# Windowed attention before a softmax-gated layer: four groups of partitions hold half a sequence of one head instead of a quarter of two

## The chip, the cores and the metric

The kernel runs on one core of one Trainium2 chip. The metric is the device time of one execution in microseconds (us); the kernel before takes 502.13 us, the median of three runs (501.51 to 502.85).

## The reference, cut to what matters

There are 8 batches of 8 heads, 576 positions and 64 numbers per head. Each query sees 32 keys behind it: the nearest 32 in heads 0 to 3, every fourth of the last 128 in heads 4 to 7. The attention output, 4608 rows of 512, then goes through a dense layer to 1024, a softmax-weighted gate, a normalisation and a dense layer back to 512.

```python
mask_plain = (rel >= 0) & (rel < window)                                   # window = 32
mask_dil = (rel >= 0) & (rel < window * dilation) & (rel % dilation == 0)  # dilation = 4
attn = softmax(where(mask, q @ k.T / 8, -1e9)); x = attn @ v               # per batch and head
h = x @ w_in;  e = exp(h - max(h));  solu = h * e / sum(e)
out = ((solu - mean) / sqrt(var + 1e-6) * g_ln) @ w_out
```

The host reorders the positions of the dilated heads by their remainder by four, so both kinds of head become a window of 32 neighbours, in the dilated case with three class borders at which the window is cut.

## The kernel before, in words

The attention is done in 32 units, one for each batch and pair of heads (`NUNIT`). Units with n % 4 below 2 are plain, the others dilated. The dense layers are done in 36 tiles of 128 tokens. The order of the work on each engine is written out by hand: the string `OPENING` gives it for the first part, `STEP` and `AMID` for tiles 6 to 15, `PAIR` and its variants for the pairs of tiles after that. A word such as `S5` is "the scores of unit 5"; each word issues its instructions on its engine at that place. All loads go through SP's queue in the order of the words.

A unit's words are these. `q` and `v` load its operands. `S` (`scores`, L235 to L259) multiplies queries and keys on TensorE. The 576 queries of a head are cut into four groups of 144, each group into five blocks of 32 (the last block of a group is half used), and a block is multiplied with 64 keys. Head h lies in partitions 64h to 64h+63 of both operands, group c is written to partitions 32c to 32c+31, head h to its own PSUM bank: 5 x 2 x 4 = 40 matmuls, each 64 rows by 32 columns of the array, with 64 columns streamed. For units 0 to 9 (`PE_MASK`) two matmuls with an identity first write the mask into the banks; for the others `mask` adds it on VectorE (L266). Then come `max`, `sub`, `exp`, `sum`, `inv`, `norm` and `turn` (a 32x32 transpose), all on tiles of 128 x 640. `sub` is on GpSimd except in the early units, `exp` on ScalarE, `norm` on GpSimd for units 0 to 9, the rest on VectorE. `V` (`attend`, L318 to L337) multiplies the turned probabilities with the values: one matmul for each 32-key block (six in a group, five where the first is left out), each group and each head, 32 rows by 64 columns of the array, with 16 to 64 columns streamed; group c writes bank 4 + c. A plain unit has 48 of them, a dilated one 40. `xh` and `xl` copy the result out of PSUM (L366, L368, L385).

The scores of units 0 to 4 use banks 2 and 3, which the dense layer's odd tiles use too; those of later units use columns 144 to 463 of banks 6 and 7, whose first 144 columns belong to `V`.

The profile shows two records for each fp32 matmul of `S` and `V`, and two weight loads: an fp32 matmul is done in two passes with the same operands.

The lines of `S` and `V` that set which part of the array works:

```python
for i in range(NS):                      # S
    for h in range(2):
        for c in range(NG):
            out=ps[WIN * c : WIN * c + WIN, h, WQ * i : WQ * i + WQ]
            lhsT=qt[D * h : D * h + D, q0 : q0 + WIN]
for i in range(first, NV):               # V
    for c in range(NG):
        for h in range(2):
            out=ps_x[D * h : D * h + D, c, c0 : c0 + k1 - k0]
            lhsT=vt[WIN * c : WIN * c + WIN, i, D * h : D * h + D]
```

Of the kernel before, what the change touches and what calls it, by code (L numbers as in the profile page):

```python
# [9 lines left out]
F32 = mybir.dt.float32  # L10
# [19 lines left out]
NG = P // WIN  # L30
GQ = S // NG
NS = -(-GQ // WIN)
NV = NS + 1
SPAN = GQ * (NG - 1) + WIN * NS
RING = 2 * S
# [14 lines left out]
OPENING = (  # L50
# [72 lines left out]
LAST_BANKS = {NTILE - 3: 0, NTILE - 1: 1}  # L123
OFFSET = {'qt2': 48, 'kt2': 32, 'vt2': 48, 'qt3': 48, 'kt3': 48, 'vt3': 48}
SLOTS = "t0 t1 t2 t3 raw4 raw5 tp t0 t1 t2 t3 raw4 raw5 tp t3 tp".split()
MERGED = 5
SHIFT = {}
# [3 lines left out]
def windowed_attention_then_solu_kernel(  # L131
# [38 lines left out]
    banks = psum.tile([P, 8, 512], F32, name="banks")  # L170
    ps_x = banks[:, 4:8, 0:GQ]

# [9 lines left out]
    def ps_s(n):
        if n < MERGED:
            return banks[:, 2:4, 0 : NS * WQ]
        return banks[:, 6:8, GQ : GQ + NS * WQ]

# [9 lines left out]

    setup.tile([P, 48], F32, name="before_mag")
    loaded = {}

    def load_qk(n):  # L200

        if n >= NUNIT:
            return
        qt = units.tile([P, SPAN], F32, name=f"qt{buf(n)}", bufs=1)
        kt = units.tile([P, WIN + SPAN], F32, name=f"kt{buf(n)}", bufs=1)
# [29 lines left out]
    def scores(n):  # L235

        qt, kt = loaded[n]["q"], loaded[n]["k"]
        dil = int(n % NPAIR >= NPAIR // 2)
        ps = ps_s(n)
        st[n] = {"ps": ps.rearrange("p h (s w) -> p h s w", w=WQ)}  # L240
        on_pe = n in PE_MASK
        if on_pe:
            for h in range(2):
                nc.tensor.matmul(  # L244
                    out=ps[:, h, :], lhsT=id_bf, rhs=mask_sb[:, dil, :],
                    start=True, stop=False, skip_group_check=True,
                )
        for i in range(NS):
            for h in range(2):
                for c in range(NG):  # L250
                    q0 = GQ * c + WIN * i
                    nc.tensor.matmul(  # L252
                        out=ps[WIN * c : WIN * c + WIN, h, WQ * i : WQ * i + WQ],
                        lhsT=qt[D * h : D * h + D, q0 : q0 + WIN],
                        rhs=kt[D * h : D * h + D, q0 : q0 + WQ],
                        start=not on_pe,
                        stop=True,
                        skip_group_check=True,
                    )  # L259

    def soft_mask(n):
        if n in PE_MASK:
            return
        dil = int(n % NPAIR >= NPAIR // 2)
        sm = st[n]["sm"] = att.tile([P, 2, NS, WQ], F32, name=f"sm{n % 2}")
        nc.vector.tensor_tensor(  # L266
            out=sm.rearrange("p h s w -> p h (s w)"), in0=ps_s(n),
            in1=mask_sb[:, dil, :].unsqueeze(1).broadcast_to([P, 2, NS * WQ]),
            op=ALU.add,
        )  # L270

    def wide(x):
        return x.unsqueeze(3).broadcast_to([P, 2, NS, WQ])

    def soft_max(n):
        mx = st[n]["mx"] = small.tile([P, 2, NS], F32, name="mx")
        src = st[n]["ps"] if n in PE_MASK else st[n]["sm"]
        nc.vector.tensor_reduce(out=mx, in_=src, axis=AX.X, op=ALU.max)  # L278

    def soft_copy(n):  # L280
        sm = st[n]["sm"] = att.tile([P, 2, NS, WQ], F32, name=f"sm{n % 2}")
        nc.scalar.copy(out=sm, in_=st[n]["ps"])

# [27 lines left out]
    def turn(n):  # L311

        pt = st[n]["pt"] = att.tile([P, 2, NS * WQ], F32, name=f"pt{n % 2}")
        nc.vector.transpose(
            out=pt.rearrange("p h w -> p (h w)"), in_=st[n]["sm"].rearrange("p h s w -> p (h s w)")
        )
# [531 lines left out]
    def conv_lo(b):  # L848
# [149 lines left out]
```

## Time and profile before

| | |
|---|---|
| time, median of three runs | 502.13 us |
| span of the profiled execution | 501.3 us |
| busy: TensorE matmuls / weight loads | 471.7 / 379.3 us |
| busy: VectorE, ScalarE, GpSimd | 351.9, 289.1, 295.7 us |
| moved by DMA | 94.07 MB, 188 GB/s on average |

The span goes from the first to the last instruction of the profiled execution; the page gives no other time of that execution, and its span lies 0.8 us below the median of the runs. In the views, PE is TensorE's matmuls, PEld its weight loads, DVE is VectorE, ACT ScalarE, POOL GpSimd, SP the engine that issues the loads. PEclk is the share of TensorE's full clock that was granted (1.00 is 2.4 GHz, 0.50 is 1.2 GHz).

### The profile page before, as it was taken

The page shows a single profiled execution, that of the slowest core. Times are in us where ns is not written, and L with a number is a line of the kernel's source. Part 1 is how long each engine was busy: PE and PEld are TensorE (multiplying, and loading weights), DVE is VectorE, ACT ScalarE, POOL GpSimd, SP SyncE. Part 2 cuts the span into 40 slices and gives each one's busy share as a digit, 9 for nine tenths or more (in the row PEclk, how much of TensorE's full clock was granted, in tenths as well). Part 3 has the DMA queues.
Part 4 walks back from the last instruction along what each step waited for, and adds up shares of the span by engine and source line. Part 5 has one row for each costly group of instructions (what it writes and reads, how often), then busy time and mean ns, then how long its engine had stood idle before and what let it go on. Part 6 is the DMA issues. An engine that isn't in the chain of part 4 may idle for free.

```text
span 501.3 us, 16598 instructions
## 1 busy us (share of the span) xinstructions
PE 471.7 (94%) x7088; PEld 379.3 (76%) x7088; DVE 351.9 (70%) x619; ACT 289.1 (58%) x481; POOL 295.7 (59%) x367
## 2 busy tenths in 40 slices
PE   3449988999999999999999999999999999999997
PEld 2337766888887888878778787878787888888876
DVE  3998897768446788787868686868676864445562
ACT  3756986645233445444457575757575767666552
POOL 0463774575344665778976666665757555766440
PEclk9999997999999999999999999999999999999999
DMA  8999637554347555565667677776765545454461
GB/s 283 349 377 346 190 78 252 150 177 154 112 130 226 179 174 162 171 194 169 200 170 221 199 218 205 214 209 211 212 211 164 161 129 147 104 157 141 109 181 70
DMA packets 50905, 94.07 MB, mean 188 GB/s; under 512 B 5648, under 2 KB 25616, under 8 KB 50832
## 3 DMA queue, kind: packets, MB, share of 16 engines
q1 hardware_dynamic: 49968, 92.30, 59.8%
q8 instruction: 55, 0.90, 0.7%
q10 hardware_dynamic: 864, 0.72, 0.4%
q14 instruction: 18, 0.15, 0.1%
HBM read 59.97 MB, written 28.31 MB: 176 GB/s over the span
## 4 chain that ended last, share of the span: by engine, by line
PE 87%; DVE 8%; DMA 2%; issue 2%; ACT 1%; SPq 0%; DVEq 0%; ACTq 0%
PE banks L528 37%; PE banks L758 20%; PE banks L398 17%; PE banks L330 6%; PE banks L252 6%; DMA t<-w_in 1%; PE banks L549 1%; DVE mag L821 1%; DVE mag L836 1%; DVE t L433 1%; DVE mx L278 1%; DVE rs L299 1%; DVE low L828 1%; DMA mid<-t 1%; PE banks L244 0%
## 5 line engine op out<-in xcount | busy, mean ns | idle before, releaser
L528 PE MATMUL banks<-w_o,th 128*128 128x512 f32 x560 | 174.9, 393 | 0.0
L528 PEld LDWEIGHTS banks<-w_o,th 128*128 128x128 f32 x560 | 103.6, 188 | 21.8 <-ACT th L513 0.4
L519 POOL TENSOR_TENSOR tl<-t,th 128x512 fp32r<-128x512 f32 x68 | 88.1, 1310 | 48.4 <-ACT th L513 48.1
L528 PE MATMUL banks<-w_o,tl 128*128 128x512 f32 x280 | 109.3, 390 | 0.0
L398 PE MATMUL banks<-w_i,x_hi 128*128 128x512 f32 x256 | 84.0, 410 | 0.1
L528 PEld LDWEIGHTS banks<-w_o,tl 128*128 128x128 f32 x280 | 52.5, 188 | 11.6 <-DVE tl L519 0.4
L513 ACT CAST th<-t 128x512 fp32r<-128x512 f32 x72 | 43.5, 620 | 28.3 <-DVE t L505 14.6
L398 PEld LDWEIGHTS banks<-w_i,x_hi 128*128 128x128 f32 x256 | 48.3, 195 | 11.1 <-DVE mu L433 0.2
L505 DVE STREAM_TRANSPOSE t<-raw 128x512 f32<-128x512 f32 x72 | 47.4, 687 | 10.4 <-DMA raw<-mid 10.3
L398 PE MATMUL banks<-w_i,x_lo 128*128 128x512 f32 x128 | 51.3, 401 | 0.0
L330 PEld LDWEIGHTS banks<-pt,vt 32*64 32x64 f32 x2816 | 35.2, 137 | 20.9 <-issue 10.5
L449 ACT ACTIVATE e<-t 128x1024 f32<-128x1024 f32 x35 | 37.0, 1057 | 21.4 <-DVE t L445 21.0
L330 PE MATMUL banks<-pt,vt 32*64 32x64 f32 (+3 forms) x2816 | 38.7, 234 | 9.9 <-DMA vt<-vw 4.0
L291 POOL TENSOR_TENSOR sm<-sm,mx 128x640 f32<-128x640 f32 x25 | 31.6, 1263 | 24.2 <-DVE mx L278 17.0
L266 DVE TENSOR_TENSOR sm<-banks,packed 128x640 f32<-128x640 f32 x22 | 18.1, 823 | 38.8 <-PE banks L252 38.8
L295 ACT ACTIVATE sm<-sm 128x640 f32<-128x640 f32 x32 | 23.6, 738 | 35.0 <-POOL sm L291 32.4
L252 PEld LDWEIGHTS banks<-kt,qt 64*32 64x32 f32 x2560 | 29.9, 113 | 16.1 <-issue 9.8
L540 ACT ACTIVATE ob<-banks,rstd 128x512 f32<-128x512 f32 x35 | 24.0, 686 | 27.9 <-issue 16.7
L252 PE MATMUL banks<-kt,qt 64*32 64x64 f32 x2560 | 35.7, 241 | 4.0 <-DMA qt<-qT 3.2
L782 DVE CUSTOM_DVE_ANT_0 t<-banks,t 128x512 f32<-128x512 f32 x30 | 20.7, 690 | 22.4 <-PE banks L758 17.0
L776 ACT COPY t<-banks 128x512 f32<-128x512 f32 x30 | 17.6, 588 | 30.3 <-PE banks L758 30.3
L442 ACT ACTIVATE t<-t,mu 128x1024 f32<-128x1024 f32 x23 | 26.4, 1149 | 11.0 <-DVE mu L441 11.0
(156 smaller groups left out, 880.0 us busy)
## 6 DMA issues: line engine op xcount, KB each, us to landing
mid<-t SPq DMA_DIRECT2D x140, 128.0 KB, 2.4
raw<-mid SPq DMA_DIRECT2D x34, 512.0 KB, 3.8
vt<-vw SPq DMA_DIRECT2D x32, 384.0 KB, 3.9
kt<-kT SPq DMA_DIRECT2D x32, 312.0 KB, 4.0
qt<-qT SPq DMA_DIRECT2D x32, 296.0 KB, 4.3
out<-ob SPq DMA_DIRECT2D x35, 256.0 KB, 2.6
x_hi<-x SPq DMA_DIRECT2D x12, 288.0 KB, 3.6
t<-w_in SPq DMA_DIRECT2D x5, 512.0 KB, 8.4
```

The source lines that it names most:

```text
L252: nc.tensor.matmul(out=ps[WIN * c : WIN * c + WIN, h, WQ * i : WQ * i + WQ], lhsT=qt[D * h : D * h + D, q0 : q0 + WIN], rhs=kt[D * h : D * ...
L291: eng.tensor_tensor(out=st[n]["sm"], in0=st[n]["sm"], in1=wide(mx), op=ALU.subtract)
L330: nc.tensor.matmul(out=ps_x[D * h : D * h + D, c, c0 : c0 + k1 - k0], lhsT=vt[WIN * c : WIN * c + WIN, i, D * h : D * h + D], rhs=pt[WIN * ...
L398: nc.tensor.matmul(out=ps_h(i)[:, half], lhsT=a[:, kt, xs], rhs=w_i[:, kt, half, part, :], start=(kt == 0 and k == 0), stop=(kt == KT - 1 ...
L442: nc.scalar.activation(out=dst, in_=src, func=AF.Identity, bias=mu, scale=1.0)
L449: nc.scalar.activation(out=e, in_=t, func=AF.Square, accum_out=per_tile(i, "sq"))
L505: nc.vector.transpose(out=turned(i)[:, cut(c)].rearrange("p k (a r) -> p k a r", r=WIN), in_=ms[i]["mv"].rearrange("p (a k s) -> p k a s", ...
L513: nc.scalar.copy(out=ms[i]["th"][:, cut(c)], in_=turned(i)[:, cut(c)])
L519: eng.tensor_tensor(out=ms[i]["tl"][:, cut(c)], in0=turned(i)[:, cut(c)], in1=ms[i]["th"][:, cut(c)].bitcast(F32), op=ALU.subtract,)
L528: nc.tensor.matmul(out=ps_o(i), lhsT=a[:, f, :], rhs=w_o[:, f, part, :], start=(f == 0 and k == 0), stop=(f == FT - 1 and k == 2), skip_gr ...
L540: nc.scalar.activation(out=ob, in_=ps_o(i), func=AF.Copy, scale=rstd)
L758: nc.tensor.matmul(out=banks[:, bank], lhsT=left(pa, kt), rhs=right(pb, kt), start=j in (1, 2, 5) and kt == 0 and k == 0, stop=kt == 1 and ...
```

## The change: nine whole blocks of one head in each group

The 576 queries of a head are now cut into two halves of 288, which are nine whole blocks of 32. Group c of 32 partitions holds half c % 2 of head c // 2. So a unit's score tile is 128 x 576 instead of 128 x 640. `S` has 9 x 2 x 2 = 36 matmuls instead of 40. `V` has 38 in a plain unit instead of 48 (ten key blocks in the second half, nine in the first, whose first block lies before the sequence), and 36 in a dilated unit instead of 40. Head h in partitions 64h to 64h+63 now meets only groups 2h and 2h+1.

The scores of all units use columns 192 to 511 of bank 6 (five blocks) and 0 to 255 of bank 7 (four). The value products use columns 0 to 287 of banks 4 and 5, one bank for each half. The mask is no longer shared by the two heads, so the packed constants grow from 392 to 648 columns; they are loaded in two pieces, the identity and the plain mask first (352 columns), the dilated mask and the gains (296 columns) by a new word `rest` between `S1` and `q2`. The padding of queries, keys and values goes: q has 576 columns instead of 592, k 608 instead of 624, v 640 instead of 768.

```diff
-GQ = S // NG
-NS = -(-GQ // WIN)
+GQ = S // 2
+NS = GQ // WIN
+FIRST_BANK = 5
-    "pack q0 S0 w0 q1 max0 sub0 low0 abs0 w3 exp0 abs3 S1 q2 clamp0 low3 sign0 sum0 w2 inv0 "
+    "pack q0 S0 w0 q1 max0 sub0 low0 abs0 w3 exp0 abs3 S1 rest q2 clamp0 low3 sign0 sum0 w2 inv0 "
-    ps_x = banks[:, 4:8, 0:GQ]
+    ps_x = banks[:, 4:6, 0:GQ]
+    s0 = 7 * 512 - FIRST_BANK * WQ
+    ps_s = banks.rearrange("p a b -> p (a b)")[:, s0 : s0 + NS * WQ]
-        vt = units.tile([P, NV, 2 * D], F32, name=f"vt{buf(n)}", bufs=1)
+        vt = units.tile([P, NV, D], F32, name=f"vt{buf(n)}", bufs=1)
...
         for i in range(NS):
-            for h in range(2):
-                for c in range(NG):
-                    q0 = GQ * c + WIN * i
+            for half in range(2):
+                for h in range(2):
+                    c = 2 * h + half
+                    q0 = GQ * half + WIN * i
                     nc.tensor.matmul(
-                        out=ps[WIN * c : WIN * c + WIN, h, WQ * i : WQ * i + WQ],
+                        out=ps_s[WIN * c : WIN * c + WIN, WQ * i : WQ * i + WQ],
...
-        for i in range(first, NV):
-            k0, k1 = max(WQ * i - WIN, 0), min(WQ * i + WIN, WQ * NS - WQ + WIN + GQ % WIN)
+        for i in range(NV):
+            k0, k1 = max(WQ * i - WIN, 0), min(WQ * i + WIN, NS * WQ)
             c0 = WIN * max(i - 1, 0)
-            for c in range(NG):
+            for half in range(2):
+                first = int(dil or half == 0)
+                if i < first:
+                    continue
                 for h in range(2):
+                    c = 2 * h + half
                     nc.tensor.matmul(
-                        out=ps_x[D * h : D * h + D, c, c0 : c0 + k1 - k0],
-                        lhsT=vt[WIN * c : WIN * c + WIN, i, D * h : D * h + D],
-                        rhs=pt[WIN * c : WIN * c + WIN, h, k0:k1],
+                        out=ps_x[D * h : D * h + D, half, c0 : c0 + k1 - k0],
+                        lhsT=vt[WIN * c : WIN * c + WIN, i, :],
+                        rhs=pt[WIN * c : WIN * c + WIN, k0:k1],
...
-        "pack": lambda _: nc.sync.dma_start(out=packed, in_=pack),
+        "pack": lambda _: nc.sync.dma_start(out=packed[:, 0:early], in_=pack[:, 0:early]),
+        "rest": lambda _: nc.sync.dma_start(out=packed[:, early:], in_=pack[:, early:]),
```

## Rows read from the trace of the kernel before

**Rows 1.** The page, part 4: the chain that ended last, by engine.

```profile
PE 87%; DVE 8%; DMA 2%; issue 2%; ACT 1%; SPq 0%; DVEq 0%; ACTq 0%
```

**Rows 2.** Windows: stretch, its length, busy us (instructions) of PE, PEld, DVE, ACT, POOL; PEclk, DMA, GB/s.

```profile
25.00:50.00 25.00, 17.62 (x455) 14.11 (x456) 22.84 (x36) 15.57 (x26) 12.12 (x10) 1.00 0.97 362
50.00:75.00 25.00, 22.86 (x581) 17.91 (x580) 23.05 (x40) 23.02 (x37) 18.39 (x28) 0.99 0.47 134
75.00:100.00 25.00, 23.23 (x244) 18.50 (x243) 18.77 (x32) 16.72 (x28) 13.59 (x16) 0.87 0.64 199
300.00:325.00 25.00, 25.00 (x410) 20.15 (x408) 18.48 (x38) 16.06 (x29) 16.50 (x22) 1.00 0.73 211
```

**Rows 3.** Chain in order of time, 300 to 345 us: start, length, what.

```profile
299.93 1.01 PE banks L330 x70
...
303.89 0.97 PE banks L252 x64
...
325.24 1.13 PE banks L330 x75
```

**Rows 4.** Waits of PE after 90 us, all of them: total us, times, longest.

```profile
PE banks L549 <- DVE tl L519: 0.2, 1, 0.2
PE banks L330 <- issue: 0.2, 1, 0.2
```

**Rows 5.** Timeline of PE around one `S`: start, first start to last end, records.

```profile
380.14 1.04 PE L252 MATMUL banks<-kt,qt 64*32 64x64 f32 x80
381.11 0.50 PE L758 MATMUL banks<-tp,w_i 128*128 128x512 f32 x1
```

**Rows 6.** Windows on L252, same `S`: PE and PEld records begun by each end; PEclk.

```profile
380.13:380.19 0.06, 0.05 (x8) 0.05 (x12) 1.00 0.76 307
380.13:380.22 0.09, 0.08 (x8) 0.08 (x16) 1.00 0.76 307
380.13:380.27 0.14, 0.13 (x16) 0.13 (x23) 1.00 0.76 307
380.13:380.33 0.20, 0.19 (x24) 0.19 (x32) 1.00 0.87 353
```

**Rows 7.** Windows on L252, an `S` at half clock.

```profile
84.89:84.95 0.06, 0.05 (x8) 0.05 (x12) 0.50 0.01 0
84.89:85.10 0.21, 0.20 (x16) 0.20 (x24) 0.50 0.00 0
84.89:85.20 0.31, 0.30 (x24) 0.30 (x32) 0.50 0.00 0
```

**Rows 8.** Windows on L330, a plain `V`.

```profile
388.00:388.08 0.08, 0.07 (x8) 0.07 (x11) 1.00 0.00 0
388.00:388.14 0.14, 0.13 (x16) 0.13 (x20) 1.00 0.00 0
388.00:388.22 0.22, 0.21 (x24) 0.21 (x31) 1.00 0.00 0
```

**Rows 9.** Groups of instructions by line: busy us, mean ns, idle before and releaser.

```profile
L266 DVE TENSOR_TENSOR sm<-banks,packed 128x640 f32<-128x640 f32 x22 | 18.1, 823 | 38.8 <-PE banks L252 38.8
L278 DVE TENSOR_REDUCE mx<-sm 128x10 f32<-128x640 f32 x22 | 18.0, 820 | 0.8
L314 DVE STREAM_TRANSPOSE pt<-sm 128x640 f32<-128x640 f32 x32 | 26.8, 837 | 0.9 <-POOL sm L309 0.6
L505 DVE STREAM_TRANSPOSE t<-raw 128x512 f32<-128x512 f32 x72 | 47.4, 687 | 10.4 <-DMA raw<-mid 10.3
```

**Rows 10.** Chain in order of time, 0 to 112 us, four of 129 pieces.

```profile
33.11 1.41 PE banks L252 x80
...
36.87 1.46 PE banks L330 x62
...
63.01 0.84 DVE mx L278
...
84.97 1.33 PE banks L252 x78
```

**Rows 11.** DMA issues: times, KB each, median us to landing.

```profile
vt<-vw SPq DMA_DIRECT2D x32, 384.0 KB, 3.9
...
packed<-pack SPq DMA_DIRECT2D x1, 196.0 KB, 2.4
```

More of the change, by code (lines that the diff above doesn't have):

```diff
@@ L123 @@
 LAST_BANKS = {NTILE - 3: 0, NTILE - 1: 1}
[L124 removed]
+OFFSET = {'qt2': 48, 'kt2': 48, 'vt2': 112, 'qt3': 48, 'kt3': 48, 'vt3': 112}
 SLOTS = "t0 t1 t2 t3 raw4 raw5 tp t0 t1 t2 t3 raw4 raw5 tp t3 tp".split()
[L126 removed]
 SHIFT = {}
@@ L161, in windowed_attention_then_solu_kernel @@
     id_bf = packed[:, 0 : P // 2].bitcast(BF16)
+    early = P // 2 + NS * WQ // 2
     mask_sb = packed[:, P // 2 : P // 2 + NS * WQ].bitcast(BF16).rearrange("p (d c) -> p d c", d=2)
@@ L180, in ps_o @@
         return banks[:, LAST_BANKS.get(i, i % 2 if i < PAIRED - 2 else 3)]
[L182 to L185, printed above, removed]
     nc.vector.memset(mhalf, -0.5)
@@ L195, in buf @@
         return n % 4 if n < 12 else n % 2
-    setup.tile([P, 48], F32, name="before_mag")
+    setup.tile([P, 112], F32, name="before_mag")
+    units.tile([P, 64], F32, name="before_units", bufs=1)
     loaded = {}
@@ L203, in load_qk @@
             return
-        qt = units.tile([P, SPAN], F32, name=f"qt{buf(n)}", bufs=1)
-        kt = units.tile([P, WIN + SPAN], F32, name=f"kt{buf(n)}", bufs=1)
+        qt = units.tile([P, S], F32, name=f"qt{buf(n)}", bufs=1)
+        kt = units.tile([P, WIN + S], F32, name=f"kt{buf(n)}", bufs=1)
         nc.sync.dma_start(out=kt, in_=kT[n])
@@ L238, in scores @@
         dil = int(n % NPAIR >= NPAIR // 2)
-        ps = ps_s(n)
-        st[n] = {"ps": ps.rearrange("p h (s w) -> p h s w", w=WQ)}
+        st[n] = {"ps": ps_s.rearrange("p (s w) -> p s w", w=WQ)}
         on_pe = n in PE_MASK
         if on_pe:
-            for h in range(2):
+            for cols in (slice(0, FIRST_BANK * WQ), slice(FIRST_BANK * WQ, NS * WQ)):
                 nc.tensor.matmul(
-                    out=ps[:, h, :], lhsT=id_bf, rhs=mask_sb[:, dil, :],
+                    out=ps_s[:, cols], lhsT=id_bf, rhs=mask_sb[:, dil, cols],
                     start=True, stop=False, skip_group_check=True,
@@ L264, in soft_mask @@
         dil = int(n % NPAIR >= NPAIR // 2)
-        sm = st[n]["sm"] = att.tile([P, 2, NS, WQ], F32, name=f"sm{n % 2}")
+        sm = st[n]["sm"] = att.tile([P, NS, WQ], F32, name=f"sm{n % 2}")
         nc.vector.tensor_tensor(
-            out=sm.rearrange("p h s w -> p h (s w)"), in0=ps_s(n),
-            in1=mask_sb[:, dil, :].unsqueeze(1).broadcast_to([P, 2, NS * WQ]),
-            op=ALU.add,
+            out=sm.rearrange("p s w -> p (s w)"), in0=ps_s, in1=mask_sb[:, dil, :], op=ALU.add
         )
     def wide(x):
-        return x.unsqueeze(3).broadcast_to([P, 2, NS, WQ])
+        return x.unsqueeze(2).broadcast_to([P, NS, WQ])
     def soft_max(n):
-        mx = st[n]["mx"] = small.tile([P, 2, NS], F32, name="mx")
+        mx = st[n]["mx"] = small.tile([P, NS], F32, name="mx")
         src = st[n]["ps"] if n in PE_MASK else st[n]["sm"]
@@ L280, in soft_copy @@
     def soft_copy(n):
-        sm = st[n]["sm"] = att.tile([P, 2, NS, WQ], F32, name=f"sm{n % 2}")
+        sm = st[n]["sm"] = att.tile([P, NS, WQ], F32, name=f"sm{n % 2}")
         nc.scalar.copy(out=sm, in_=st[n]["ps"])
@@ L286, in soft_sub @@
         if n in PE_MASK and n not in ACT_SCORES:
-            sm = st[n]["sm"] = att.tile([P, 2, NS, WQ], F32, name=f"sm{n % 2}")
+            sm = st[n]["sm"] = att.tile([P, NS, WQ], F32, name=f"sm{n % 2}")
             nc.vector.tensor_tensor(out=sm, in0=st[n]["ps"], in1=wide(mx), op=ALU.subtract)
@@ L297, in soft_sum @@
     def soft_sum(n):
-        rs = st[n]["rs"] = small.tile([P, 2, NS], F32, name="rs")
+        rs = st[n]["rs"] = small.tile([P, NS], F32, name="rs")
         nc.vector.tensor_reduce(out=rs, in_=st[n]["sm"], axis=AX.X, op=ALU.add)
@@ L311, in turn @@
     def turn(n):
[L313 to L316, printed above, removed]
+        pt = st[n]["pt"] = att.tile([P, NS * WQ], F32, name=f"pt{n % 2}")
+        nc.vector.transpose(out=pt, in_=st[n]["sm"].rearrange("p s w -> p (s w)"))
     def attend(n):
@@ L344, in x_order @@
         if n % NPAIR < NPAIR // 2:
-            return x.rearrange("p (c i) -> p c i", c=NG)
-        return x.rearrange("p (i c) -> p i c", c=NG)
+            return x.rearrange("p (b i) -> p b i", b=2)
+        return x.rearrange("p (i b c) -> p i b c", b=2, c=2)
     def x_view(n, x):
@@ L351, in from_v @@
     def from_v(n):
-        return ps_x if n % NPAIR < NPAIR // 2 else ps_x.rearrange("p c i -> p i c")
+        if n % NPAIR < NPAIR // 2:
+            return ps_x
+        return ps_x.rearrange("p b (c i) -> p i b c", c=2)
     def whole(n):
@@ L561, in moe_out_part @@
         else:
-            ob = att.tile([P, 2, NS, WQ], F32, name=f"sm{int(on_act)}")
-            ob = ob.rearrange("p h s w -> p (h s w)")
+            ob = att.tile([P, NS, WQ], F32, name=f"sm{int(on_act)}")
+            ob = ob.rearrange("p s w -> p (s w)")
         rows, rstd = out[i * P : i * P + P, :], ms[i]["rstd"]
@@ L613, in in_unit @@
     def in_unit(name):
-        shape = {"q": [P, SPAN], "k": [P, WIN + SPAN], "v": [P, NV, 2 * D], "x": [P, S]}[name[0]]
+        shape = {"q": [P, S], "k": [P, WIN + S], "v": [P, NV, D], "x": [P, S]}[name[0]]
         pool = att if name == "x" else units
@@ L936, in _mask @@
         for p in range(P):
-            q0 = GQ * (p // WIN) + WIN * s
+            q0 = GQ * (p // WIN % 2) + WIN * s
             q = q0 + p % WIN
             k = q0 - WIN + c
-            ok = (q >= S) | ((k >= 0) & (q - k >= 0) & (q - k < WIN))
+            ok = (k >= 0) & (q - k >= 0) & (q - k < WIN)
             m[p, 0, s, ok] = 0.0
-            m[p, 1, s, ok & ((q >= S) | (k // CLS == q // CLS))] = 0.0
+            m[p, 1, s, ok & (k // CLS == q // CLS)] = 0.0
     return m.reshape(P, 2, NS * WQ)
@@ L961 @@
     q, k, v = (np.concatenate([a[:, :hh], _class_major(a[:, hh:])], axis=1) for a in (q, k, v))
-    qT = np.zeros((NUNIT, P, SPAN), q.dtype)
-    qT[:, :, :S] = q.reshape(NUNIT, 2, S, D).transpose(0, 1, 3, 2).reshape(NUNIT, P, S)
-    kT = np.zeros((NUNIT, P, WIN + SPAN), k.dtype)
-    kT[:, :, WIN : WIN + S] = k.reshape(NUNIT, 2, S, D).transpose(0, 1, 3, 2).reshape(NUNIT, P, S)
-    vp = np.zeros((NUNIT, WIN + SPAN, 2, D), v.dtype)
-    vp[:, WIN : WIN + S] = v.reshape(NUNIT, 2, S, D).transpose(0, 2, 1, 3)
-    vw = np.stack([vp[:, GQ * c : GQ * c + WIN * NV] for c in range(NG)], axis=1)
-    vw = vw.reshape(NUNIT, NG, NV, WIN, 2 * D).transpose(0, 1, 3, 2, 4)
-    vw = np.ascontiguousarray(vw).reshape(NUNIT, P, NV, 2 * D)
+    qT = q.reshape(NUNIT, 2, S, D).transpose(0, 1, 3, 2).reshape(NUNIT, P, S)
+    qT = np.ascontiguousarray(qT)
+    kT = np.zeros((NUNIT, P, WIN + S), k.dtype)
+    kT[:, :, WIN:] = k.reshape(NUNIT, 2, S, D).transpose(0, 1, 3, 2).reshape(NUNIT, P, S)
+    vp = np.zeros((NUNIT, 2, WIN + S, D), v.dtype)
+    vp[:, :, WIN:] = v.reshape(NUNIT, 2, S, D)
+    vw = np.stack([vp[:, :, GQ * c : GQ * c + WIN * NV] for c in range(2)], axis=2)
+    vw = vw.reshape(NUNIT, NG, NV, WIN, D).transpose(0, 1, 3, 2, 4)
+    vw = np.ascontiguousarray(vw).reshape(NUNIT, P, NV, D)
     arrays = {
```

6 lines of the change are left out of this document (1 added, 5 removed).

## The prediction

> **What bounds the kernel now.** Read the chain of waits first: TensorE holds 87% of it [rows 1]. Then the windows, since the share is an average: between 25 and 75 us VectorE is busy 22.8 to 23.1 of 25 us while TensorE has idle time, and up to 50 us the DMA engines are 97% busy; from 100 us on TensorE is busy all the time at the full clock [rows 2]. The waits say the same: after 90 us TensorE waits 0.4 us in all [rows 4]. So from 100 us to the last tiles a nanosecond more or less on TensorE is one of the total, and work saved on VectorE, ScalarE or GpSimd is worth nothing. In this stretch lie 22 `S` (units 10 to 31) and 24 `V` (units 8 to 31, twelve plain, twelve dilated). On the chain an `S` takes 0.97 us, a dilated `V` 1.01 (80 records), a plain one 1.13 (96 records) [rows 3]. What they cost afterwards is the whole question.
>
> **What an `S` is made of.** 40 matmuls in two passes give 80 records [rows 5]. Eight records begin in the first 50 ns; then none until 80 ns, sixteen by 130, twenty-four by 190 [rows 6]: groups of eight, about 56 ns apart. Eight is the number of array parts the code uses (two halves of rows times four groups of columns). At the half clock the same steps are about 107 ns (8, 16 and 24 records by 0.06, 0.21 and 0.31 us) [rows 7]. So the step follows the array's clock, not the supply of instructions. I read it so: a part takes one record every 56 ns, and the passes of one matmul, on one part, come one after the other. The rows don't name the parts, so this is a reading; its alternative is rival A. At eight parts 80 records would need 10 steps, 0.56 us; the unit needs 0.97, because the first burst, which was queued beforehand, is followed by a slower supply. Its price: a plain `V` has 8 matmuls more than a dilated one and takes 0.12 us longer [rows 3], 15 ns a matmul. Today supply and latency bind, not the parts.
>
> **`S` after.** Head h now meets only column groups 2h and 2h+1, so four parts are used instead of eight, for nine matmuls each, 18 records. The first record streams after its weight load, 80 - 53 = 27 ns (53 is a step less its handover, half of 107); then 17 steps of 56 are 0.95 us, and the fourth part lies 0.02 behind: the last record starts at 1.00 us. Now it starts about 0.82 (records end at 1.04, one lasts 0.22) and the next product starts at 0.97, 0.15 later [rows 5]. So an `S` takes 1.15 instead of 0.97; with no stagger and 53 ns steps 1.09. Value +0.175 us, bounds +0.12 and +0.19. The four matmuls saved would give 0.06 if supply still bound; it doesn't.
>
> **`V` after.** Same cut: four parts instead of eight. In a `V` the steps are 55 to 60 ns (8, 16, 24 records by 80, 140 and 220 ns, the first with narrow edges) [rows 8]. A plain unit's second half has ten matmuls, 20 records: first load 0.05, 19 steps of 57 are 1.08, tail 0.15: 1.28 against 1.13. A dilated one has nine: 0.05 + 17 x 0.057 + 0.02 + 0.15 = 1.19 against 1.01. Narrow edge blocks may take a little off. Value +0.16, bounds +0.12 and +0.19.
>
> Sum after 100 us: 22 x 0.175 + 24 x 0.16 = 3.9 + 3.8 = **+7.7 us**; by the bounds 46 x 0.12 = 5.5 to 46 x 0.19 = 8.7.
>
> **The softmax.** Tiles shrink from 640 to 576 columns. A transpose falls by 64/128 of the difference between 640 and 512 columns, (837 - 687)/2 = 75 ns; additions and maxima, 820 ns now, by about as much [rows 9]. That is 0.3 us of VectorE for each unit, hidden after 100 us, where VectorE is busy 18.5 of 25 us [rows 2]; if that cover went it would be a gain. It counts in the opening: 18 such operations lie on the chain up to 84 us (one is shown [rows 10]), -1.3 us.
>
> **The opening on TensorE.** Six units run at half clock, S0 to S4 and S9; three steps of half-clock work are on the chain: S4 (1.41), V1 (1.46 after a stall) and S9 (1.33) [rows 10]. By the step of 107 an `S` becomes 0.05 + 17 x 0.107 + 0.02 + 0.25 (its tail now: 1.33 less a last start of 1.1) = 2.1: +0.75 each, +2.25 for the three. Six warm units on the chain there add 6 x 0.17 = 1.0. S0 to S3 and V0 lie beside VectorE's work, which sets that stretch; uncovered, they cost up to 4 x 0.8 = 3.2 more. Sum -1.3 + 2.25 + 1.0 = **+2.0 us**. Below: all half-clock units hidden and the loads earlier, -2; above: +5.
>
> **Loads.** A unit's v falls from 384 to 320 KB [rows 11], k and q by 8 each: 80 KB of 992 less; the constants grow from 196 to 324 KB, of which 176 go ahead. In the stretch at 362 GB/s that is 0.2 us less for each unit and 0.4 us more once. `rest` puts one more issue in SP's queue ahead of `q2` and all later loads; S2, which needs both, waits for VectorE's subtraction of unit 1 anyway. I put the sum at 0 and at -1 to +0.5 for the bounds above. After 100 us the DMA share is about 0.7 and nothing waits for it [rows 2, 4].
>
> **The banks.** Scores and values no longer share banks 6 and 7, and early scores leave banks 2 and 3. A wait that this could remove would be in TensorE's 0.4 us, so it is worth 0. Reading is not slowed by the sharing either: the mask addition from PSUM takes 823 ns, the maximum of the same size from SBUF 820 [rows 9]. The new strides of the copies out of PSUM lie on ScalarE and VectorE, beside TensorE's work.
>
> **Forecast.** 501.3 + 7.7 + 2.0 = 511.0 for the span; the median of the runs lies 0.8 above the span, so **511.8 us**. Its own range is 505 to 517.
>
> **Rivals.** A, faster: the groups of eight are a limit on records in flight, whichever part they go to, and supply still binds with four parts. For it: eight is also a plausible depth, and no row shows fewer than eight parts at work. Against it: the step doubles with the clock, and second passes would have to overlap first ones on the same part. Price, at 15 ns a matmul: `S` -0.06, plain `V` -0.15, dilated -0.06, 1.3 + 1.8 + 0.7 = -3.8 us, and -2 in the opening (softmax -1.3, fewer matmuls): 496.3 us. It decides as soon as nine matmuls on one part take under 0.8 us. The Trainium skill, TensorEngine Tiling (Array Packing), section Instruction Overhead, says a matmul carries some 60 cycles whatever its width, so that fewer matmuls would be faster by 25 ns a record. The trace doesn't agree for packed parts: 80 records in 0.97 us.
>
> B, much slower: today heads write different banks in `S`, and the four row groups different banks in `V`; afterwards both heads write one bank at once, from different rows of the array to different partitions. If such matmuls took turns, two parts would work at a time: `S` 36 steps of 56 ns and 0.2, 2.2 us; `V` about the same: +1.2 x 46 = 55, and 8 in the opening: 565 us. No row shows two row groups on one bank, for or against; that each partition has its own stretch of a bank speaks against. The same page of the Trainium skill, section Gotcha 1: PSUM Pressure, states the rule, that row tiles work into different banks and not into one at the same time; no row here can show what breaking it does.
>
> C, no change: parts overlap load and stream better when fewer work, the units cost half (+4) and the opening gives 2 to 4 back by VectorE and the loads: 502. For it: VectorE's 92% in the opening. Against: the step is already the streaming time.
>
> **Chances.** Forecast 0.80, A 0.11, B 0.05, C 0.04. To hold 8 in 10 the range takes the forecast's own and reaches part of the way to A and C: 501 to 517. About 0.3% (1.5 us) is what a measurement of this kernel can tell from no change: faster 0.12, same 0.04, slower 0.84.
>
> **What would show it.** Right: `S` at 1.09 to 1.16 us on the chain, `V` at 1.13 to 1.3, only four records in the first 50 ns until the step after, TensorE still without waits after 100 us, and the start of the steady part 0 to 4 us later. Wrong: an `S` under 0.97 (A) or above 1.5 us (B), or gaps of TensorE in the steady part.

## The result: 1.3% slower; the steady part near the forecast, the opening shorter instead of longer

The kernel after takes 509.18 us (median of 4 runs, 508.56 to 509.80), the kernel before 502.49 us beside it: a ratio of 1.0132, 95% interval 1.0098 to 1.0166. The forecast was 511.8. The profiled span goes from 501.3 to 506.8 us.

The chain by engine, then the windows and the waits of TensorE after 90 us, of the kernel after; they answer to [rows 1], [rows 2] and [rows 4].

```profile
PE 89%; DMA 6%; DVE 3%; SPq 1%; ACT 1%; issue 0%; DVEq 0%; ACTq 0%
```

```profile
25.00:50.00 25.00, 20.12 (x437) 16.39 (x441) 21.54 (x36) 16.52 (x28) 12.10 (x10) 1.00 0.98 356
50.00:75.00 25.00, 23.12 (x492) 18.68 (x482) 22.40 (x40) 22.18 (x35) 18.20 (x30) 1.00 0.51 146
75.00:100.00 25.00, 23.33 (x239) 19.02 (x238) 18.92 (x34) 17.87 (x31) 15.62 (x20) 1.00 0.58 192
300.00:325.00 25.00, 25.00 (x375) 20.10 (x375) 17.34 (x35) 15.53 (x28) 15.40 (x22) 1.00 0.65 194
```

```profile
PE banks L547 <- ACT th L511: 1.2, 1, 1.2
PE banks L547 <- DVE tl L517: 0.2, 1, 0.2
```

TensorE still does nothing but work from 100 us on. In the third window its granted clock is now 1.00, where before it was 0.87. The wait of 1.2 us is at the very end, for the last tiles; it comes again when the kernel after is run once more (1.3 us).

The chain in order of time from 300 to 345 us, after, against [rows 3] (`S` is L250, `V` L326); and windows on the line of `S` from the start of one, against [rows 6].

```profile
300.89 1.18 PE banks L326 x72
...
305.04 1.14 PE banks L250 x72
...
326.90 1.28 PE banks L326 x74
```

```profile
309.07:309.10 0.03, 0.03 (x4) 0.03 (x5) 1.00 1.42 555
309.07:309.13 0.06, 0.06 (x4) 0.06 (x8) 1.00 1.89 619
309.07:309.17 0.10, 0.10 (x8) 0.10 (x11) 1.00 1.56 538
309.07:309.22 0.15, 0.15 (x11) 0.15 (x14) 1.00 1.32 469
309.07:309.28 0.21, 0.21 (x15) 0.21 (x19) 1.00 1.30 473
```

An `S` takes 1.14 us instead of 0.97, a plain `V` 1.28 instead of 1.13, a dilated one 1.18 instead of 1.01, with fewer matmuls each. Four records begin at once where eight did, the next four by 0.10 us.

Where the steady part begins is read from the timeline: `V8`, the first unit after the opening, before and after.

```profile
103.68 1.20 PE L330 MATMUL banks<-pt,vt 32*64 32x32 f32 x96
```

```profile
100.41 1.35 PE L326 MATMUL banks<-pt,vt 32*64 32x32 f32 x76
```

So the part up to `V8` became 3.3 us shorter and the part behind it grew from 397.6 to 406.4, by 8.8 us, where 7.7 were forecast and 8.7 was the upper bound. The opening went the other way.

### The profile page after: what moved, and what is told of

It is laid out like the page before. It is cut to its first block, busy times and chain, and to the rows that moved or that the text cites. A ratio compares the mean times of both kernels' runs of the same rounds, so it can differ in the third digit from the quotient of the medians.

```text
span 506.8 us, 15186 instructions
## 1 busy us (share of the span) xinstructions
PE 481.8 (95%) x6384; PEld 391.0 (77%) x6384; DVE 340.6 (67%) x619; ACT 287.3 (57%) x481; POOL 290.8 (57%) x367
## 4 chain that ended last, share of the span: by engine, by line
PE 89%; DMA 6%; DVE 3%; SPq 1%; ACT 1%; issue 0%; DVEq 0%; ACTq 0%
PE banks L526 36%; PE banks L756 20%; PE banks L396 17%; PE banks L326 7%; PE banks L250 7%; DMA qt<-qT 3%; DMA vt<-vw 2%; PE banks L547 1%; DMA mid<-t 1%; DVE t L431 1%; DMA raw<-mid 1%; PE banks L241 0%; SPq L204 0%; DVE mx L274 0%; DVE sm L284 0%
## 5 line engine op out<-in xcount | busy, mean ns | idle before, releaser
L396 PE MATMUL banks<-w_i,x_hi 128*128 128x512 f32 x256 | 81.8, 401 | 0.3 <-DVE mu L431 0.3
L396 PEld LDWEIGHTS banks<-w_i,x_hi 128*128 128x128 f32 x256 | 47.0, 189 | 10.8 <-DVE mu L431 0.4
L326 PEld LDWEIGHTS banks<-pt,vt 32*64 32x64 f32 x2368 | 41.0, 141 | 16.9 <-issue 6.0
L326 PE MATMUL banks<-pt,vt 32*64 32x64 f32 (+1 forms) x2368 | 44.5, 227 | 6.3 <-DVE mag L819 4.4
L264 DVE TENSOR_TENSOR sm<-banks,packed 128x576 f32<-128x576 f32 x22 | 16.6, 756 | 48.8 <-PE banks L250 48.8
L250 PEld LDWEIGHTS banks<-kt,qt 64*32 64x32 f32 x2304 | 37.9, 116 | 13.8 <-issue 12.2
L250 PE MATMUL banks<-kt,qt 64*32 64x64 f32 x2304 | 43.4, 232 | 2.4 <-DMA qt<-qT 2.4
L287 POOL TENSOR_TENSOR sm<-sm,mx 128x576 f32<-128x576 f32 x25 | 28.8, 1153 | 27.3 <-DVE mx L274 20.5
L291 ACT ACTIVATE sm<-sm 128x576 f32<-128x576 f32 x32 | 21.9, 684 | 37.2 <-POOL sm L287 34.4
L422 ACT ACTIVATE e<-t,nmax 128x1024 f32<-128x1024 f32 x19 | 21.9, 1152 | 20.1 <-DVE nmax L787 19.5
```

The costliest lines, as they stand in the source:

```text
L250: nc.tensor.matmul(out=ps_s[WIN * c : WIN * c + WIN, WQ * i : WQ * i + WQ], lhsT=qt[D * h : D * h + D, q0 : q0 + WIN], rhs=kt[D * h : D * ...
L291: nc.scalar.activation(out=sm, in_=sm, func=AF.Exp, scale=0.125)
L326: nc.tensor.matmul(out=ps_x[D * h : D * h + D, half, c0 : c0 + k1 - k0], lhsT=vt[WIN * c : WIN * c + WIN, i, :], rhs=pt[WIN * c : WIN * c ...
L396: nc.tensor.matmul(out=ps_h(i)[:, half], lhsT=a[:, kt, xs], rhs=w_i[:, kt, half, part, :], start=(kt == 0 and k == 0), stop=(kt == KT - 1 ...
```

## The experiments

All ratios are to the kernel before, run on the same chip.

**Four parts without the change.** The kernel before with its counts of matmuls and tiles, but operands read so that only four of the eight array parts work (neither this run nor the next computes the attention).

```diff
-    lhsT=qt[D * h : D * h + D, q0 : q0 + WIN],
-    rhs=kt[D * h : D * h + D, q0 : q0 + WQ],
+    lhsT=qt[D * (c // 2) : D * (c // 2) + D, q0 : q0 + WIN],
+    rhs=kt[D * (c // 2) : D * (c // 2) + D, q0 : q0 + WQ],
...
+    g = WIN * (2 * h + c % 2)
-    lhsT=vt[WIN * c : WIN * c + WIN, i, D * h : D * h + D],
-    rhs=pt[WIN * c : WIN * c + WIN, h, k0:k1],
+    lhsT=vt[g : g + WIN, i, D * h : D * h + D],
+    rhs=pt[g : g + WIN, h, k0:k1],
```

> The kernel before with its 40 score matmuls and 48 or 40 value matmuls, but each reads rows that put it on one of four array parts instead of eight (scores from the row half of group c // 2, values from the row group 2h + c % 2; the output holds other products). Parts theory: an S takes 1.26 us instead of 0.97 (10 matmuls on a part, 20 steps of 56 ns), a plain V 1.50 instead of 1.13, a dilated V 1.28 instead of 1.01; 22 x 0.29 + 12 x 0.37 + 12 x 0.27 = +14 us after 100 us and about +3 before, 519 us. Rival (a limit on records in flight or on supply, whichever part they go to): S 0.97, V 1.13 and 1.01 as before, 502 us.

Measured 517.58 us, ratio 1.0289 (1.0238 to 1.0341). Its chain in order of time:

```profile
123.83 1.52 PE banks L331 x96
...
136.45 1.28 PE banks L331 x80
...
146.12 1.25 PE banks L252 x80
```

These are a plain `V`, a dilated `V` and an `S`. Same matmuls, same tiles, half the parts: each unit is 0.27 to 0.39 us longer than in the kernel before.

**Eight parts with the change.** The kernel after with every second block reading the other head's rows; in `V` these blocks also write other banks (6 and 7).

```diff
+    r = h ^ (i % 2)
+    s = i // 2 if i % 2 == 0 else FIRST_BANK + i // 2
-    out=ps_s[WIN * c : WIN * c + WIN, WQ * i : WQ * i + WQ],
-    lhsT=qt[D * h : D * h + D, q0 : q0 + WIN],
-    rhs=kt[D * h : D * h + D, q0 : q0 + WQ],
+    out=ps_s[WIN * c : WIN * c + WIN, WQ * s : WQ * s + WQ],
+    lhsT=qt[D * r : D * r + D, q0 : q0 + WIN],
+    rhs=kt[D * r : D * r + D, q0 : q0 + WQ],
...
+    x, x0 = ps_x[:, half], c0
+    if i % 2 == 0:
+        c, x0 = c ^ 2, c0 % 128
+        x = banks[:, 6 + half, 256 * half : 256 * half + 160]
```

> The changed kernel with its 36 score matmuls and 38 or 36 value matmuls, but every second block reads the other head's rows and goes to another bank, so that eight array parts are used (the output holds other products); both heads still write one bank at once in the scores. Parts theory: supply binds again, S 0.89 us instead of 1.14, plain V 0.98 instead of 1.28, dilated V 0.97 instead of 1.18; 22 x 0.25 + 12 x 0.30 + 12 x 0.21 = -11.6 us after 100 us, -1 to -2 before, 496.5 us against 509. Rival (two row halves on one bank take turns in part, whatever the parts): S stays near 1.14, the time at 503 to 509.

Measured 494.34 us, ratio 0.9834 (0.9783 to 0.9885); the chain:

```profile
143.00 0.96 PE banks L332 x59
...
152.35 0.90 PE banks L252 x58
156.22 0.97 PE banks L332 x54
```

The two together settle rival A: with the parts halved and the counts kept, units grow; with the parts back, the fewer matmuls pay.

**Both kernels once more**, for the opening.

> The kernel before once more, for a second profile. If the two drops of the clock at 74.5 and 84.8 us and the stall of 2 us in V1 belong to its order of work, they come again and V8 starts at 103.7 us; if they are chance, V8 starts 1 to 4 us earlier.

> The changed kernel once more. S 1.14, V 1.28 and 1.18 us again; if the opening's gain is the change's own, no drop of the clock between 39 and 500 us and V8 at 100.4 us; if chance, drops come in some profiles and V8 is at 102 to 104. Time 509 us, 1.013 of before.

Before: 505.8 us (one run), after: 507.96 us, ratio 1.0109 (1.0068 to 1.0150). `V8` starts at 105.95 and 99.69 us. So the opening's gain is 3.3 us in one pair of profiles and 6.3 in the other; the two profiles of before lie further apart than those of after. After `V8` it is 398.1 and 406.4 us.

**The softmax as wide as before.** The kernel after with the softmax of units 0 to 9 on 640 columns (and one more small mask product for each).

```diff
-    sm = st[n]["sm"] = att.tile([P, NS, WQ], F32, name=f"sm{n % 2}")
+    sm = st[n]["sm"] = sm_tile(n)
...
+    def sm_tile(n):
+        sm = att.tile([P, NS + 1, WQ], F32, name=f"sm{n % 2}")
+        return sm if n in PE_MASK else sm[:, 1:]
```

> The changed kernel, but the softmax of units 0 to 9 (maximum, subtraction, exponential, sum, scaling, transpose) runs on 128 x 640 again, with one idle block ahead, and one small mask matmul more on TensorE; matmuls of S and V are the changed kernel's. Theory 1 (the narrower tiles give the opening what the step of my sum said): V8 starts 1.3 us later than in the changed kernel, 101 to 101.7 us, time +1.3. Theory 2 (they give nearly all of the 3 to 6 us by which the opening is shorter): V8 at 103.5 to 106, time 512 or more. Theory 3 (the opening's gain is loads or the clock): V8 at 100.4 within 0.5.

Measured 510.88 us, ratio 1.0164 (1.0115 to 1.0214); `V8` at 102.39, 2.0 and 2.7 us later than in the two profiles of after: between what theories 1 and 2 said. Not all of it need be the softmax: TensorE also stops 0.57 us for "issue" at 39 us here.

**Loads as large as before.** The kernel after with q, k and v padded to the sizes of before.

```diff
+    QC, KC, VC = 592, 624, 12
-    qt = units.tile([P, S], F32, name=f"qt{buf(n)}", bufs=1)
+    qt = units.tile([P, QC], F32, name=f"qt{buf(n)}", bufs=1)
...
+    vw = np.pad(vw, ((0, 0), (0, 0), (0, VC - NV), (0, 0)))
```

> The changed kernel with the loads of before: q, k and v padded to 592, 624 and 768 columns (992 KB a unit instead of 912). If the smaller loads give the opening its gain: V8 2 to 4 us later than 100 us, time 511 to 513. If not, as my sum has it: within 1 us of the changed kernel, 509.

Measured 510.30 us, ratio 1.0152 (1.0112 to 1.0192); `V8` at 100.95, 0.5 and 1.3 us later than in the two profiles of after.

**The kernel before without its idle gaps.** Idle 128 x 512 products fill TensorE's gaps ahead of `V7` and `S9`.

```diff
-    "... turn7 xl5 V6 var2 xh6 e3 "
+    "... turn7 xl5 V6 fill6 var2 xh6 e3 "
-    "... join12 join13 abs15 S9 "
+    "... join12 join13 abs15 fill5 S9 "
+    def fill(count):
+        for _ in range(count):
+            nc.tensor.matmul(
+                out=banks[:, 0], lhsT=x_hi[:, 0, 0:P], rhs=w_i[:, 0, 0, 0, :], start=True, stop=True
+            )
```

> The kernel before with idle products on TensorE (read by nobody) in its two gaps, six between V6 and V7 and five ahead of S9. Theory (the two drops of the clock follow from TensorE's idle gaps there and cost about 3 us): no drop between 40 and 500 us, V8 at 100.5 to 101.5 us instead of 103.7 or 105.9, time 499.5. Rival (the drops are not from these gaps): drops at 74 and 85 us again, V8 at 103.7 or later, time 502.5.

Measured 501.62 us, ratio 0.9975 (0.9950 to 0.9999), a smaller gain than the 3 us expected; `V8` at 101.72. The windows from 74 to 78 and from 84 to 88 us of the kernel before, then of this one (columns as in [rows 2]):

```profile
74.00:78.00 4.00, 3.91 (x12) 3.06 (x11) 3.79 (x11) 4.00 (x8) 2.86 (x8) 0.57 0.99 279
...
84.00:88.00 4.00, 3.49 (x86) 2.74 (x86) 3.97 (x8) 3.16 (x6) 0.00 (x0) 0.60 0.67 225
```

```profile
74.00:78.00 4.00, 3.91 (x93) 3.32 (x94) 3.79 (x9) 4.00 (x6) 3.02 (x9) 1.00 0.77 190
...
84.00:88.00 4.00, 4.00 (x94) 3.24 (x93) 3.93 (x9) 3.26 (x6) 0.00 (x0) 1.00 0.79 257
```

Before, TensorE stands idle 1.99 us ahead of `V7` and 1.77 ahead of `S9`, and behind both the granted clock is at its lower level, 1.2 GHz, for a while, in the repeat too; with the gaps filled (0.41 and 0.42 us left) it stays at 1.00. In the kernel after the first gap is 1.55 us (`V6` lasts 0.17 us longer, and `V7` starts 0.27 sooner behind the start of `V6`), the second 1.67, and the clock stays at 1.00 in both profiles.

Not every execution of the kernel before seems to lose its clock there. Of its 19 runs beside this experiment, 11 have a mean granted clock of 0.993 or less and take 502.6 to 507.1 us (median 504.6); the other 8, at 0.997 or more, take 499.8 to 503.2 (median 501.7). All ten with the gaps filled are at 0.999 or more, with a median of 501.6. So the clock costs about 3 us where it falls, as it did in both profiles, and 1.3 us over all runs by the ratio; where it falls in the runs without a profile is not shown.

**More instructions.** The kernel after with as many matmuls in units 0 to 7 as before has: tiny idle ones, whose results nobody reads, behind each `S` and `V`.

```diff
+    if n < 8:
+        for j in range(4):
+            idle_product(j, qt[D * (j // 2) : D * (j // 2) + D, 0:WIN],
+                         kt[D * (j // 2) : D * (j // 2) + D, 0:2])
...
+    if n < 8:
+        for j in range(4 if dil else 10):
+            c = j % 4
+            idle_product(c, vt[WIN * c : WIN * c + WIN, 1, 0:WIN],
+                         pt[WIN * c : WIN * c + WIN, 0:2])
```

> The kernel after, with as many matmuls in units 0 to 7 as the kernel before has: four tiny idle ones (two columns) behind each S, ten behind each plain V and four behind each dilated one, on the four parts. By the parts they cost at most 0.1 to 0.2 us a unit. Theory (TensorE's instructions arrive in loads of 16 KB, one for 128 records, about 6.5 us apart while the loads fill the DMA engines, and the kernel before outruns them in V1 and V2): the stall put down to issue in V1 or V2 comes back, 1 to 3 us, and V8 starts 2 to 4 us later than in the kernel after, at 102 to 104 us. Rival (the stall has to do with the loads of v or the banks): no such stall, V8 at 100 to 101.5 us.

Measured 510.55 us, ratio 1.0144 (1.0097 to 1.0191); `V8` at 103.40. The timeline of TensorE from 26 to 39 us, `V1`, `S4` and `V2` with what lies between them: the kernel before, the kernel after, this one (idle time before a row in brackets).

```profile
27.18 1.15 PE L330 MATMUL banks<-pt,vt 32*64 32x32 f32 x52 [2.65 <-DMA vt<-vw]
30.07 0.95 PE L330 MATMUL banks<-pt,vt 32*64 32x64 f32 x44 [1.74 <-issue]
32.40 0.69 PE L244 MATMUL banks<-packed 128*128 128x320 bf16 x2 [1.38 <-DVE sm L288]
33.11 1.41 PE L252 MATMUL banks<-kt,qt 64*32 64x64 f32 x80
34.45 0.36 PE L330 MATMUL banks<-pt,vt 32*64 32x64 f32 x1
36.87 1.46 PE L330 MATMUL banks<-pt,vt 32*64 32x64 f32 x79 [2.06 <-issue]
```

```profile
27.76 2.35 PE L326 MATMUL banks<-pt,vt 32*64 32x32 f32 x76 [4.35 <-DVE mag L819]
...
32.86 2.14 PE L250 MATMUL banks<-kt,qt 64*32 64x64 f32 x72 [0.23 <-DMA qt<-qT]
34.94 2.15 PE L326 MATMUL banks<-pt,vt 32*64 32x64 f32 x72
```

```profile
26.14 1.76 PE L337 MATMUL banks<-pt,vt 32*64 32x32 f32 x52 [1.46 <-DMA vt<-vw]
30.27 0.86 PE L337 MATMUL banks<-pt,vt 32*64 32x64 f32 x24 [2.37 <-issue]
...
35.11 0.36 PE L337 MATMUL banks<-pt,vt 32*64 32x64 f32 x1
36.48 2.14 PE L337 MATMUL banks<-pt,vt 32*64 32x64 f32 x71 [1.01 <-issue]
```

Read the counts. Before, TensorE stops inside `V1` after its 52nd record, and again after the first of `V2`: 44 + 2 + 80 + 1 = 127 records later. With the counts made equal the kernel after stops at the same two records, though its layout, its loads and its banks are the changed ones. The queue of instructions on the profile's page fits that number (before, then after):

```profile
q8 instruction: 55, 0.90, 0.7%
```

```profile
q8 instruction: 50, 0.82, 0.7%
```

That is 55 loads of 16 KB for 7088 matmul records before and 50 for 6384 after, 129 and 128 records to a load. In the trace of before such loads begin at 27.7 and 34.5 us, beside stops that end at 30.07 and 36.87, while the DMA engines are 97% busy [rows 2]. So TensorE outran its own instructions. The run with four parts and the counts of before has no such stop, but it comes to these records later (`V1` starts at 28.98 instead of 27.18, `V2` at 36.36 instead of 34.45). The rival is out; the tiny products themselves cost at most 0.41 + 0.28 + 0.28 us by then, and `V3` starts 1.8 to 2.5 us later than in the profiles of after (43.87 against 42.06 and 41.4). The times of the whole do not tell the two kernels apart: 510.55 us here against 509.18 and 507.96.

**Eight parts for the real computation.** Group c = 2 half + p takes five blocks of head p and four of the other head, so the changed layout uses all eight parts, at 42 and 40 matmuls for a `V`, four banks and two or three copies out.

```diff
-    for i in range(NS):
+    for i in (0, 5, 1, 6, 2, 7, 3, 8, 4):
         for half in range(2):
-            for h in range(2):
-                c = 2 * h + half
+            for p in range(2):
+                c, h = 2 * half + p, p ^ (i >= N5)
...
+    for run, length, s0, ps in ((0, N5, 0, ps_5), (1, N4, N5, ps_4)):
+        h, first = p ^ run, int(run == 0 and (dil or half == 0))
```

> Whole blocks in each group as in the change, but each group holds five blocks of one head and four of the other (group c = 2 half + p: blocks 0 to 4 of the half from head p, blocks 5 to 8 from the other head), so eight array parts are used and every part writes its own bank; the full computation. S 36 matmuls, V 42 (plain) or 40 (dilated), values 352 KB a unit, copies out of PSUM in two or three pieces instead of one. Parts theory: S 0.90 us, V 1.06 and 1.05, after 100 us -1.8 against the kernel before; the opening about 4 us shorter than before, as in the changed kernel and the eight-part run: 496 us, faster than both. Rival (the pieces of the copies or the shared banks give waits on TensorE): TensorE idle after 100 us, 500 us or more.

Measured 506.96 us, ratio 1.0074 (1.0036 to 1.0112). The units were as expected (0.90, 1.06, 1.06), but the sum was not: it takes 399.0 us after `V8`, 1.4 more than the kernel before instead of 1.8 less, 2.0 us of it in the wait at the end. And `V8` starts at 106.13. The waits of TensorE up to 107 us, three of nine:

```profile
PE banks L243 <- DVE x_lo L392: 3.5, 1, 3.5
PE banks L330 <- issue: 3.2, 1, 3.2
...
PE banks L243 <- ACT x_hi L367: 2.0, 1, 2.0
```

**The same, placed anew,** with and without idle products ahead of `V7` and `S9`: the values of a half in one stretch, two copies out (the cut is against the version above).

```diff
-    ps_x = banks[:, 4:8].rearrange("p (b k) c -> p b (k c)", b=2)
-    ps_5, ps_4 = ps_x[:, :, 0 : WIN * N5], ps_x[:, :, 768 : 768 + WIN * N4]
-    s0 = 7 * 512 - FIRST_BANK * WQ
+    s0 = 6 * 512 - FIRST_BANK * WQ
+    v0 = [(5 + 2 * half) * 512 - WIN * N5 for half in range(2)]
+    ps_v = [flat[:, v : v + GQ] for v in v0]
```

> The real computation on eight parts, with scores and value products placed so that the copies of one unit no longer hold up the scores of the next: each half of the values lies in one unbroken stretch (columns 352 to 511 of one bank and 0 to 127 of the next), scores in columns 192 to 511 of bank 5 and 0 to 255 of bank 6, so a copy out is two instructions and touches no score; 6 idle products between V6 and V7 and 5 ahead of S9 keep TensorE at work there. Parts theory: S 0.90 us, V 1.06, V8 starts at 99 to 101 us, no wait on L243 in the opening, about 398 us after V8, so 497 to 500 us, below both kernels. Rival (the second copy instruction of each unit costs ScalarE and VectorE what the parts give): V8 at 104 or later, 503 to 506 us.

> The same without the idle products. If the clock falls in the gap ahead of V7 or S9 as it does in the kernel before, V8 comes 1.5 to 3 us later than with them; if the gaps stay as short as in the kernel after (1.55 and 1.67 us), no difference: 497 to 500 us.

Measured 503.95 us, ratio 1.0015 (0.9986 to 1.0044), and 505.27 us, ratio 1.0032 (1.0001 to 1.0062): a miss. `V8` starts at 103.26 and 103.83, then 397.5 and 396.9 us. Mask products still wait 3.6 and 1.6 us for the copies (3.5 and 1.6 without idle products), though no column is shared, only a bank; and the stop at the instructions is there in both, inside `V2`. With idle products:

```profile
34.25 1.40 PE L337 MATMUL banks<-pt,vt 32*64 32x32 f32 x65
39.18 0.64 PE L337 MATMUL banks<-pt,vt 32*64 32x64 f32 x15 [3.53 <-issue]
```

**Four parts first, then eight.** Units 0 to 7 as in the kernel after (fewest matmuls, one copy, no shared bank), 8 to 31 on eight parts (the cut is against the version above).

```diff
-    c, h = 2 * half + p, p ^ (i >= N5)
+    c, h = 2 * half + p, p ^ (i >= N5 and n >= FOUR)
...
+    if n < FOUR:
+        for i in range(NS + 1):
...
+                        out=ps_four[D * h : D * h + D, half, c0 : c0 + k1 - k0],
...
+    if n < FOUR:
+        return [(y, ps_four)]
```

> The real computation in a mixture: units 0 to 7 as in the kernel after (four parts, fewest matmuls, one copy instruction), units 8 to 31 on eight parts as in the two-copies version. If the opening's loss there is due to its additional matmuls and copies, V8 starts at 99.5 to 101 us as in the kernel after, then 397 us: a span of 497 to 498 us, ratio 0.988 to 0.993, faster than both kernels. Rival (the change of layout at unit 8 makes S8 wait for the copies of V7, or the clock falls): V8 at 102 or later, ratio 0.995 to 1.0.

Measured 498.03 us, ratio 0.9913 (0.9875 to 0.9950): faster than both kernels. `V8` from its timeline, then `S` from its chain:

```profile
99.35 1.13 PE L356 MATMUL banks<-pt,vt 32*64 32x32 f32 x84
```

```profile
140.94 0.90 PE banks L259 x58
```

The opening is that of after, without a stop for instructions in `V1` or `V2`; behind `V8` it takes 396.9 us instead of 406.4, with one stop of 1.27 us put down to issue in an `S` at 380 us.

## Why the prediction was right, and where it was wrong

**Units on four parts: right.** `S` was to be 1.15 and is 1.14, plain `V` 1.28 and 1.28, dilated 1.19 and 1.18. The sum of +7.7 us is 22 x 0.17 + 12 x 0.15 + 12 x 0.17 = 7.6 by the measured rows. The two experiments on the number of parts show the cause: a part takes one record each 56 ns, and at half the parts it, not supply, sets the length. The other 1.2 us behind `V8` fit the wait at the end, which was not foreseen: with more instructions in units 0 to 7 it is not there, and the part behind `V8` takes 405.2 us. What decides it is not found.

**Rival B: out.** Both heads now write one bank at once, and four records still begin within 0.03 us, with no unit near 2.2 us. The Trainium skill, TensorEngine Tiling (Array Packing), section Gotcha 1: PSUM Pressure, says that row tiles cannot use one bank at the same time; the trace doesn't agree for tiles that write different partitions of the bank (1.14 us for an `S`, not 2.2).

**The opening, +2.0 us: wrong in sign and outside its bounds (-2 to +5).** It is -3.3 and -6.3 in the two pairs of profiles, and by the medians about 6.7 - 8.8 = -2.1; the steady part was to start 0 to 4 us later. Rival C had the opening right (2 to 4 us back) and the units wrong. That 509.18 lies only 2.6 us from the forecast is in part luck: the steady part's 1.1 us too much make up for some of the opening's 4.1 too little. The starts of `V3` and `V8` part it:

| us | `V3` | `V8` | between |
|---|---|---|---|
| before, its repeat | 43.56, 44.6 | 103.68, 105.95 | 60.1, 61.4 |
| before, gaps filled | 44.5 | 101.72 | 57.2 |
| after, its repeat | 42.06, 41.4 | 100.41, 99.69 | 58.4, 58.3 |
| after, more instructions | 43.87 | 103.40 | 59.5 |

- Up to `V3`, 1.5 and 3.2 us are gained. The failed step is "V1 (1.46 after a stall)" (that row is `V2` by the order of the words): it costed the streaming behind the stall and passed over the stall, put down to "issue", as if it would stay. The chain of before, then of after:

```profile
31.62 0.74 DVE sm L288
...
34.81 2.06 issue
```

```profile
32.86 2.14 PE banks L250 x72
35.01 2.08 PE banks L326 x72
```

Only the stop of 2.06 us in `V2` is on the chain; the one of 1.74 in `V1` lies beside VectorE's work, which `S4` waits for. Without the 2.06 `V2` ends at 37.1 instead of 38.3, although `S4` and `V2` themselves grew by 0.73 and 0.33: so in this pair the fewer matmuls account for the gain, by way of the instructions. In the second pair the stops are even, 1.22 us in `V2` before and 1.25 in the dense layer after. Its 3.2 us come from `S4`, which starts 1.3 us sooner, and from lengths as at the lower clock, which last until 43 us before and 35 after; why these differ is not shown.

- `S4` became 2.1 us as worked out. That it runs at the lower clock level is read from its steps, not from the clock column, which is 1.00 there in both kernels: 8, 16 and 24 records of the `S4` of before begin by 0.05, 0.20 and 0.30 us, as in [rows 7], and in the run with the wide softmax the column is 0.50 over an `S4` of 2.15 us.
- From `V3` to `V8`, without the clock, the change costs 58.3 - 57.2 = 1.1 us, as "six warm units" had it (+1.0). But the clock counts 2.9 and 4.2 us in the two profiles of before. The step "S9 (1.33)" took the half clock as given, for a slower `S9` to come; instead `S9` runs at the full clock in 1.14 us. And the sum had no term for the dense layer's products behind the two gaps, 24 each on the chain: 7.35 and 6.57 us before, 5.73 and 5.67 after. In an execution of before whose clock does not fall, this part of the gain is not there.
- The softmax was sized at -1.3 us; with its old width back `V8` comes 2.0 to 2.7 us later. Each operation fell by 65 to 67 ns, near the 75 of the estimate (see the rows below), so the count of 18 does not give it; GpSimd's subtraction (1263 to 1153 ns) and ScalarE's exponential (738 to 684) fell as well and were not in it, which may be the rest, with the stop of 0.57 us.
- The loads were put at 0 and were worth 0.5 to 1.3 us, the upper part of it beyond the bound of -1.

VectorE's groups after, against [rows 9]:

```profile
L310 DVE STREAM_TRANSPOSE pt<-sm 128x576 f32<-128x576 f32 x32 | 24.7, 771 | 0.6 <-POOL sm L305 0.2
L264 DVE TENSOR_TENSOR sm<-banks,packed 128x576 f32<-128x576 f32 x22 | 16.6, 756 | 48.8 <-PE banks L250 48.8
L274 DVE TENSOR_REDUCE mx<-sm 128x9 f32<-128x576 f32 x22 | 16.6, 755 | 0.8
```

These parts come from single profiles and overlap: softmax, loads and instructions all act ahead of `V3`, so they are not to be added.

**What stays open.** When the clock falls behind a gap in the kernel before and when not, and the wait at the end. The new banks and copies out were not tried by themselves, so a share of theirs in the opening is neither shown nor excluded; and of the runs of after that were not profiled, some have a mean granted clock of 0.983 to 0.990, without a row that says where. That the mask products' waits in the eight-part versions come from the shared bank is only argued.

## What to carry to other kernels

Count the parts of the array that a packed loop keeps busy, and the records on the busiest of them, before counting matmuls: fewer matmuls on half the parts were slower, and the same ones on all the parts faster. Where loads fill the DMA engines, an engine's own instructions are one more load: idle time put down to "issue" in such a stretch is worth as many microseconds as any wait where it lies on the chain (2.06 in `V2`, nothing in `V1`), and fewer instructions can remove it. A clock that is low behind a gap is not a property of the stage; ask whether the change lengthens or closes the gap.

## What the runs showed that was not expected

- TensorE's instructions come in loads of 16 KB, 128 matmul records each; in every profile with a stop put down to issue in `V2` it came ahead of the same record, the 604th from the start: in seven profiles, of four different layouts. In the repeat of after the 604th lies in the dense layer, and the stop (1.25 us) is there, as with the wide softmax (0.57) and with eight parts in the changed kernel (0.79).
- The granted clock went to its lower level at the gap ahead of `V7` where TensorE had stood idle 1.99 and 1.97 us (before), 2.64 (first eight-part version) and 1.69 (eight parts with the change). It stayed at 1.00 with 1.55 (after, twice; padded loads; four parts without the change), 1.66 (wide softmax) and 0.41 (filled). Ahead of `S9` it fell with 1.77 us (before) and stayed with 1.80 (wide softmax), so the length of the gap alone does not decide.
- Eight parts on 36 matmuls need 0.90 us for an `S`, 36 x 2 / 8 = 9 steps of 56 ns and 0.4 us more: there, as in the kernel before, something other than the parts binds; I take it to be the supply of queued matmuls.
